# Splitting float64 dense weights and scaling softmax rows in a fused attention and two-layer MoE kernel: which engine does three of its steps

## The chip, the cores and the metric

One core of one Trainium2 chip runs the whole program. The metric is the device time of one execution in microseconds; below it the profile's own span is named where it is used. The engines have short names in the profile: PE (matmul), DVE (VectorE), ACT (ScalarE), POOL (GpSimd), SP (which issues most of the DMAs).

## The reference

```python
# attention: q, k, v are (4, 8, 576, 64); causal window of 128, ALiBi-like bias
scores = scale * q @ k.T; scores = where(mask, scores + bias, -1e9)
attn = exp(scores - max); attn = attn / (attn.sum(-1) + 1e-9)
x = (attn @ v)                      # as (2304, 512)
# dense layer: w_in (512, 2048) and w_out (2048, 512) are float64
h = x @ w_in; g = h * sigmoid(1.702 * h); x = g @ w_out
# sparse layer: 8 experts, one per token by argmax(x @ w_gate), skipped where x @ w_skip <= 0
y = gate * (relu(x @ w1[e]) @ w2[e]); out = x + y on the tokens that are not skipped
```

## The kernel before

The 2304 tokens are 18 tiles of 128 rows; two tiles make a chunk of 256 columns for the dense layer. The dense layer's hidden width is 16 slices f of 128, and each slice of weights is held as a high and a low part in the matmul's fp32 format, so that a product is three matmul passes (high x high, high x low, low x high).

**Weights of the dense layer.** They arrive as float64, read as pairs of 32-bit words. `issue` loads slice f of w_in and w_out into one of four staging tiles `stg` (SP's queue), and `tick` turns a staged slice into a pair of tiles h (high) and l (low). There are 21 such units: slices 0 to 10 whole (128 partitions x 1024) and slices 11 to 15 in two halves (128 x 512). In `tick` the steps are, in this order: ACT takes the absolute value of the high words into a scratch tile (L508); the low words are scaled by 2 to the power -29 (L510 on POOL for the slices of the tuple `LOP`, five of them, L513 on ACT for the others); DVE clamps (L514), shifts and masks (L516), combines the sign bit (L518) and adds the low words as integers (L520); ACT copies the float32 value, rounded, to h (L522); POOL subtracts h from the value and writes l (L523). At its end `tick` issues up to two more loads. All 21 units are done in the first part of the run, during the first tiles' attention and the first two chunks' dense layer.

**Attention.** `job_s` makes the scores of four heads of a tile: matmuls, masking on DVE (L318), a running minimum with the bias (L340, DVE), four exponentials with their sums (L345, ACT), the sum plus 1e-9 and its reciprocal (L347, L348, DVE) and the scaling of the four blocks by it. For tiles 0 to 3 (`full(t)`) the scaling is four instructions of 128 x 128 on POOL (L351), 32 in all; for the others it is one broadcast multiply on POOL (L354). `job_pt` transposes the scaled rows on PE (L364), copies them on ACT (L289 or L371) and cuts the two triangles on POOL (L376, L380). `job_pv` multiplies by v and writes the dense layer's input xT (ACT L411, DVE L412).

**Dense layer.** `mm1` multiplies xT by w_in (L610), applies the activation (ACT L615, DVE L616, ACT L618, DVE L619); `mm2` multiplies by w_out (L685). `main` runs them over pairs of slices and calls jobs of the next tiles in between, from the list `fill`.

**What sets the order.** The source gives an order by calls (the lists `BO`, `mix` and `fill`); a scheduler that simulates the engines with estimated durations then fixes the order in each engine's queue and puts the semaphores in. Each engine runs its queue in order. The chunks 0 and 1 run half of their slices early (`HJ`), and the rest when the later slices are ready; chunks 2 to 8 and the sparse layer come after that, with all dense weights in place.

Of the kernel before, what the change touches and what calls it, by code (L numbers as in the profile page):

```python
# [11 lines left out]
F32 = mybir.dt.float32  # L12
# [3 lines left out]
U32 = mybir.dt.uint32  # L16
I64 = mybir.dt.int64
I8 = mybir.dt.int8
AF = mybir.ActivationFunctionType
ALU = mybir.AluOpType  # L20
# [9 lines left out]
def kernel(  # L30
# [13 lines left out]
    nc = tc.nc  # L44
# [15 lines left out]
    scale = 1.0 / float(D) ** 0.5  # L60
# [105 lines left out]
    def kind_of(t):  # L166
        g = t * P
        if g % S == 0:
            return "first"
        if g // S != (g + P - 1) // S:  # L170
            return "split"
        if (g - P) // S != g // S:
            return "after"
        return "plain"
# [45 lines left out]
    def full(t):  # L220
        return t < NB
# [71 lines left out]
    def job_s(t, g):  # L293
        c = 1 if full(t) else t % 2
        kind = kind_of(t)
        if boot[0] and g == 0:
            ps = [ps_y.tile([P, 2, 2, P], F32, tag=f"y{r}", name="sps") for r in range(2)]
        else:
            ps = [ps_s.tile([P, 2, 2, P], F32, tag=f"s{r}", name="sps") for r in range(2)]
        for j in range(2):  # L300
            p = 2 * g + j
            w = slice(c, c + 1) if t == 0 else slice(0, 2)
            if full(t):
                for r in range(2):
                    nc.tensor.matmul(ps[r][:, j, w], qf[0][half[r], t, p, :],
                                     kf[0][half[r], p, max(t - 1, 0):t + 1],
                                     start=True, stop=True)
                continue
            for r in range(2):
                nc.tensor.matmul(ps[r][:, j, w], qT[t][:, r, p, :], kT[:, r, p, w],  # L310
                                 start=True, stop=False)
            for r in range(2):
                nc.tensor.matmul(ps[r][:, j, w], qlo[:, r, p, :], kT[:, r, p, w],  # L313
                                 start=False, stop=True)

        def put(p0, p1, n, data):
            for r in range(2):
                nc.vector.copy_predicated(  # L318
                    out=ps[r][p0:p1, :, c, 0:n],
                    mask=mlo[p0:p1, 0:n].unsqueeze(1).to_broadcast([p1 - p0, 2, n]),  # L320
                    data=ps[r][p0:p1, :, 1 - c, 0:n] if data is None
                    else data[p0:p1].unsqueeze(1).to_broadcast([p1 - p0, 2, n]))

        h2 = P // 2
        if kind == "first":
            put(0, P, P, big)
        elif kind == "split":
            put(0, h2, P, None)
            put(h2, P, P, big)
            for r in range(2):  # L330
                nc.vector.memset(ps[r][h2:P, :, c, 0:h2], BIG)
        else:
            put(0, P, P, None)
            if kind == "after":
                put(0, P, h2, big)
        x = ap2.tile([P, 4, P], F32, tag="e", name="e")
        mn = rp.tile([P, 4], F32, tag="mn", name="mn", bufs=2)
        sm = rp.tile([P, 4], F32, tag="sm", name="sm", bufs=2)
        for hh in range(4):
            nc.vector.tensor_tensor_reduce(out=x[:, hh, :], in0=ps[hh % 2][:, hh // 2, c, :],  # L340
                                           in1=alibi[:, 2 * g + hh // 2, :],
                                           scale=odd if hh % 2 else 1.0, scalar=3.0e38,
                                           op0=ALU.add, op1=ALU.min, accum_out=mn[:, hh:hh + 1])
        for hh in range(4):
            nc.scalar.activation(out=x[:, hh, :], in_=x[:, hh, :], func=AF.Exp, scale=-1.0,  # L345
                                 bias=mn[:, hh:hh + 1], accum_out=sm[:, hh:hh + 1])
        nc.vector.tensor_scalar_add(sm, sm, 1e-9)  # L347
        nc.vector.reciprocal(out=sm, in_=sm)  # L348
        if full(t):
            for hh in range(4):  # L350
                nc.gpsimd.tensor_scalar(out=x[:, hh, :], in0=x[:, hh, :], scalar1=sm[:, hh:hh + 1],  # L351
                                        scalar2=1.0, op0=ALU.mult, op1=ALU.mult)
        else:
            nc.gpsimd.tensor_tensor(out=x, in0=x, in1=sm.unsqueeze(2).to_broadcast([P, 4, P]),  # L354
                                    op=ALU.mult)
        eT[t, g] = x
# [58 lines left out]
    def boot_jobs(t):  # L415
        jobs = {
            "s0": lambda: job_s(t, 0),
            "s1": lambda: job_s(t, 1),
            "v": lambda: job_v(t),
            "q": lambda: t + 1 < NB and job_q(t + 1),  # L420
            "k": lambda: t + 1 < NB and job_k(t + 1),
            "p0": lambda: job_pt(t, 0),
            "p1": lambda: job_pt(t, 1),
            "o0": lambda: job_pv(t, 0),
            "o1": lambda: job_pv(t, 1),
        }
        return [jobs[z] for z in BO]
# [18 lines left out]
    NSTG = 4  # L446
    BST = (4, 7, 8)
    BO = ('s0', 's1', 'v', 'q', 'k', 'p0', 'p1', 'o0', 'o1')
    LOP = (2, 3, 4, 6, 8)
    stg = []  # L450
    stgof = []
    units = []
# [14 lines left out]
    def issue():  # L467
        i = issued[0]
        if i >= len(units) or units[i][0] >= ahead() or units[i][0] >= len(stgof):
            return  # L470
        issued[0] += 1
        f, sl = units[i]
        st = stgof[f][:, sl]
        if not wide:
            st = st.rearrange("p s d t -> p s (d t)").bitcast(F32)[:, :, 0:DM]
        staged[i] = st
        for j, s in enumerate(range(sl.start, sl.stop)):
            if s == 0:
                pat = "(k p) f t -> p k (f t)" if wide else "(k p) f -> p k f"
                dst = "p (k f) t -> p k (f t)" if wide else "p (k f) -> p k f"  # L480
                nc.sync.dma_start(
                    out=st[:, j].rearrange(dst, k=KD),
                    in_=w_in[:, f * P:(f + 1) * P].rearrange(pat, p=P))
            else:
                nc.sync.dma_start(out=st[:, j], in_=w_out[f * P:(f + 1) * P, :])

    def tick():
        i = ticked[0]
        if i >= len(units):
            return  # L490
        ticked[0] += 1
        f, sl = units[i]
        if (-1, f) not in wt:
            wt[-1, f] = wp.tile([P, 2, 2, DM], F32R, tag="w", name="w")
        h = wt[-1, f][:, 0, sl, :]
        l = wt[-1, f][:, 1, sl, :]
        x = staged.pop(i)
        if wide:
            lo, hi = x[:, :, :, 0], x[:, :, :, 1]
            if f < NFULL:  # L500
                if scr[0] is None:
                    scr[0] = wp.tile([P, 2, 2, DM], F32, tag="w", name="scr")
                c = scr[0][:, scr[1] % 2]
                scr[1] += 1
            else:
                c = yp.tile([P, 1, DM], F32, tag="b", name="wc")
            ci = c.bitcast(I32)
            nc.scalar.activation(out=c, in_=hi.bitcast(F32), func=AF.Abs)  # L508
            if f in LOP:
                nc.gpsimd.tensor_scalar(out=lo, in0=lo.bitcast(U32), scalar1=2.0 ** -29, scalar2=1.0,  # L510
                                        op0=ALU.mult, op1=ALU.mult)
            else:
                nc.scalar.activation(out=lo, in_=lo.bitcast(U32), func=AF.Copy, scale=2.0 ** -29)  # L513
            nc.vector.tensor_scalar(out=c, in0=c, scalar1=HI_MAX, scalar2=HI_MIN, op0=ALU.min,  # L514
                                    op1=ALU.max)
            nc.vector.tensor_scalar(out=ci, in0=ci, scalar1=3, scalar2=0x3FFFFFF8,  # L516
                                    op0=ALU.logical_shift_left, op1=ALU.bitwise_and)
            nc.vector.scalar_tensor_tensor(out=ci, in0=hi, scalar=-0x40000000, in1=ci,  # L518
                                           op0=ALU.bitwise_and, op1=ALU.bitwise_or)
            nc.vector.tensor_tensor(out=hi, in0=ci, in1=lo, op=ALU.add)  # L520
            x = hi.bitcast(F32)
        nc.scalar.activation(out=h, in_=x, func=AF.Copy)  # L522
        nc.gpsimd.tensor_tensor(out=l, in0=x, in1=h.bitcast(F32), op=ALU.subtract)  # L523
        for _ in range(2):
            issue()

# [825 lines left out]
```

## Time and profile before

| what | value |
|---|---|
| three runs | 809.61 us median, 808.86 to 810.9 |
| profiled execution | 808.83 us, of which the profile's span is 807.1 us |
| mean granted PE clock | 0.959 |
| busy: PE, PE weight loads | 739.3 us (92%), 656.5 us (81%) |
| busy: DVE, ACT, POOL | 520.9 us (65%), 381.7 us (47%), 382.4 us (47%) |

Busy time is the time in which an instruction of the engine is under way, waiting for a port included; it doesn't count the time before an instruction's semaphores are set. Line numbers (L523) are those of the kernel before. In a row of a stretch the busy times stand in the order PE, PE weight loads, DVE, ACT, POOL (or only the engine of the line asked for), each with its number of instructions, and behind them the granted PE clock as a share of full speed, the DMA share and GB/s. In a row of a group of instructions the name left of the arrow is what is written, the names right of it what is read.

### The profile page before, as it was taken

What the parts mean: (1) busy time and instruction counts of PE and PEld (TensorE: products, weight loads), DVE (VectorE), ACT (ScalarE), POOL (GpSimd) and SP (SyncE); (2) the same over time, 40 slices, a digit from 0 to 9 for tenths busy, and PEclk for the clock granted to TensorE, in tenths of its full rate; (3) what the DMA queues carried; (4) which work ended last, traced back from release to release, by engine and by line L of the source; (5) the groups of instructions that cost most, each with busy time, mean ns of one, the idle gap of its engine ahead of it and who ended that gap; (6) DMA issues with size and microseconds to landing.
All of it is one profiled execution on the core that took longest, in us unless ns stands there. A gap on an engine that the chain in (4) does not pass through costs nothing.

```text
span 807.1 us, 14142 instructions
## 1 busy us (share of the span) xinstructions
PE 739.3 (92%) x5087; PEld 656.5 (81%) x5087; DVE 520.9 (65%) x1195; ACT 381.7 (47%) x828; POOL 382.4 (47%) x386
## 2 busy tenths in 40 slices
PE   5658679899999999999999999999998996999994
PEld 4437469699989989999999999989987775998883
DVE  5999999954646557557557656556377537656541
ACT  4567565543444535544535544544354334545420
POOL 3699943532434326126226226227046147679540
PEclk9686889999999999999999999999999997999997
DMA  9933373111211211211211211200454177688600
GB/s 247 257 105 105 104 196 119 27 66 48 85 28 27 79 28 37 69 27 39 68 27 32 74 28 39 68 14 2 172 195 130 53 225 279 227 265 281 197 14 22
DMA packets 106151, 82.80 MB, mean 103 GB/s; under 512 B 63098, under 2 KB 83706, under 8 KB 106080
## 3 DMA queue, kind: packets, MB, share of 16 engines
q1 hardware_dynamic: 102224, 76.05, 31.6%
q0 software_dynamic: 2656, 5.67, 2.1%
q8 instruction: 41, 0.67, 0.3%
q10 hardware_dynamic: 1200, 0.17, 0.2%
q14 instruction: 30, 0.25, 0.1%
HBM read 68.98 MB, written 14.06 MB: 103 GB/s over the span
## 4 chain that ended last, share of the span: by engine, by line
PE 65%; DVE 8%; POOL 8%; issue 8%; DMA 6%; SPq 4%; ACT 1%; POOLq 0%; DVEq 0%; ACTq 0%
PE hps L610 25%; PE y L685 23%; PE ops L406 5%; POOL e L351 2%; DMA st<-in_moe_w_dram 2%; POOL w L538 2%; SPq L192 2%; PE sps L310 2%; PE hps L640 2%; PE sps L313 2%; PE pps L364 1%; PE y L670 1%; POOL w L523 1%; PE ltps L743 1%; DMA stg<-in_moe_w_in_dram 1%
## 5 line engine op out<-in xcount | busy, mean ns | idle before, releaser
L685 PE MATMUL y<-w,g 128*128 128x512 f32 x1008 | 262.1, 399 | 1.8 <-ACT g L618 1.4
L610 PE MATMUL hps<-xT,w 128*128 128x256 f32 x1728 | 240.6, 289 | 11.1 <-ACT xT L411 4.4
L610 PEld LDWEIGHTS hps<-xT,w 128*128 128x128 f32 x1728 | 225.0, 194 | 18.2 <-ACT xT L411 4.8
L685 PEld LDWEIGHTS y<-w,g 128*128 128x128 f32 x1008 | 180.7, 190 | 34.9 <-ACT g L618 1.6
L538 DVE TENSOR_TENSOR w<-st,w 128x1024 fp32r<-128x1024 f32 x38 | 66.5, 1772 | 34.5 <-ACT w L534 31.8
L616 DVE SCALAR_TENSOR_TENSOR th<-th,hps 128x512 f32<-128x512 f32 x72 | 49.3, 684 | 53.0 <-ACT th L615 52.5
L345 ACT ACTIVATE e<-e,mn 128x128 f32<-128x128 f32 x144 | 56.4, 393 | 51.1 <-DVE mn L340 50.9
L376 POOL TENSOR_SCALAR_AFFINE_SELECT pT<-pT 128x512 fp32r<-128x512 f32 (+1 forms) x64 | 46.3, 723 | 71.9 <-ACT pT L371 71.2
L615 ACT ACTIVATE th<-hps 128x512 f32<-128x512 f32 x72 | 43.0, 597 | 68.6 <-PE hps L610 55.1
L619 DVE TENSOR_TENSOR g<-th,g 128x512 fp32r<-128x512 f32 x72 | 58.5, 812 | 25.8 <-ACT g L618 24.7
L534 ACT ACTIVATE w<-st 128x1024 fp32r<-128x1024 f32 x51 | 53.2, 1057 | 35.5 <-PE y L685 12.8
L538 POOL TENSOR_TENSOR w<-st,w 128x1024 fp32r<-128x1024 f32 x26 | 67.5, 2608 | 4.3 <-ACT w L534 2.9
L618 ACT ACTIVATE g<-th 128x512 fp32r<-128x512 f32 x72 | 45.4, 631 | 40.8 <-DVE th L616 40.5
L354 POOL TENSOR_TENSOR e<-e,sm 128x512 f32<-128x512 f32 x28 | 29.2, 1044 | 70.5 <-DVE sm L348 33.7
L523 POOL TENSOR_TENSOR w<-stg,w 128x1024 fp32r<-128x1024 f32 (+1 forms) x19 | 39.9, 2102 | 19.7 <-ACT w L522 19.7
L99 POOL TENSOR_SCALAR qT<-qT 64x512 fp32r<-64x512 f32 x28 | 18.6, 663 | 62.6 <-ACT qT L240 62.0
L380 POOL TENSOR_SCALAR_AFFINE_SELECT pT<-pT 128x512 fp32r<-128x512 f32 (+1 forms) x58 | 43.7, 754 | 9.2 <-DVE pT L372 6.2
L412 DVE TENSOR_TENSOR xT<-ops,xT 64x256 fp32r<-64x256 f32 x72 | 29.7, 414 | 25.8 <-ACT xT L411 25.2
L670 PE MATMUL y<-w,g 128*128 128x512 f32 x168 | 43.9, 410 | 0.4 <-DVE o L1179 0.4
L411 ACT ACTIVATE xT<-ops 64x256 fp32r<-64x256 f32 x72 | 27.0, 375 | 34.3 <-DVE xT L412 15.9
L640 PE MATMUL hps<-w,gx 128*128 128x512 f32 x168 | 42.8, 399 | 0.2 <-ACT gx L1171 0.2
L406 PE MATMUL ops<-pT,vS 128*64 128x128 f32 x648 | 42.4, 222 | 0.0
(192 smaller groups left out, 1206.8 us busy)
## 6 DMA issues: line engine op xcount, KB each, us to landing
st<-in_moe_w_dram SPq DMA_DIRECT2D x40, 512.0 KB, 4.7
st<-in_moe_w_dram SPq DMA_DIRECT2D x48, 256.0 KB, 4.5
stg<-in_moe_w_in_dram SPq DMA_DIRECT2D x15, 512.0 KB, 4.9
stg<-in_moe_w_out_dram SPq DMA_DIRECT2D x15, 512.0 KB, 4.9
out_dram<-ys SPq DMA_DIRECT2D x18, 256.0 KB, 3.1
y_dram<-ys SPq DMA_DIRECT2D x18, 256.0 KB, 3.3
q<-in_q_dram SPq DMA_DIRECT2D x12, 256.0 KB, 2.8
k<-in_k_dram SPq DMA_DIRECT2D x12, 256.0 KB, 3.1
```

The source lines that it names most:

```text
L345: nc.scalar.activation(out=x[:, hh, :], in_=x[:, hh, :], func=AF.Exp, scale=-1.0, bias=mn[:, hh:hh + 1], accum_out=sm[:, hh:hh + 1])
L376: nc.gpsimd.affine_select(out=y[:, 0, a], in_=f32(y[:, lo, a]), pattern=[[0, 4], [1, P]], compare_op=ALU.is_ge, fill=0.0, base=0, channel_ ...
L406: nc.tensor.matmul(ps[0:64, hh % 2, hh // 2, :], vS[tt][:, a, h, :], y[:, sel, b, hh, :], start=(i == 0), stop=(i == n - 1))
L523: nc.gpsimd.tensor_tensor(out=l, in0=x, in1=h.bitcast(F32), op=ALU.subtract)
L534: nc.scalar.activation(out=h, in_=st, func=AF.Copy)
L538: eng.tensor_tensor(out=l, in0=st, in1=h.bitcast(F32), op=ALU.subtract)
L610: nc.tensor.matmul(ps[:, fi], w[:, a, 0, kk * P:(kk + 1) * P], x[:, b, kk, :], start=(i == 0), stop=(i == 3 * KD - 1))
L616: nc.vector.scalar_tensor_tensor(out=th, in0=th, scalar=1.0, in1=ps, op0=ALU.add, op1=ALU.mult)
L619: nc.vector.tensor_tensor(out=g[:, 1], in0=th, in1=g[:, 0].bitcast(F32), op=ALU.subtract)
L640: last = nc.tensor.matmul(ps, x[:, b, kk, i * P:(i + 1) * P], wa[p[0], fh, a][:, kk, :], start=(n == 0), stop=(n == 3 * KD - 1))
L670: nc.tensor.matmul(yps[p][i], g[:, a, f, :], w[:, b, f % 2, :], start=(fh == 0 and f == 0 and n == 0), stop=(fh == NH - 1 and f == 3 and n ...
L685: nc.tensor.matmul(yps[key][i], g[:, a, fi, i * P:(i + 1) * P], w[:, b, 1, :], start=(j == js[0] and fi == 0 and n == 0), stop=(j == js[-1 ...
```

## The change

Three edits. The subtraction that makes the low part l in `tick` goes from POOL to DVE (21 instructions). The scaling of the low words is on ACT for all slices (five of the wide units were on POOL). The scaling of the softmax rows of tiles 0 to 3 goes from POOL to ACT (32 instructions).

```diff
         if full(t):
             for hh in range(4):
-                nc.gpsimd.tensor_scalar(out=x[:, hh, :], in0=x[:, hh, :], scalar1=sm[:, hh:hh + 1],
-                                        scalar2=1.0, op0=ALU.mult, op1=ALU.mult)
+                nc.scalar.activation(out=x[:, hh, :], in_=x[:, hh, :], func=AF.Copy,
+                                     scale=sm[:, hh:hh + 1])
...
-    LOP = (2, 3, 4, 6, 8)
...
-            if f in LOP:
-                nc.gpsimd.tensor_scalar(out=lo, in0=lo.bitcast(U32), scalar1=2.0 ** -29, scalar2=1.0,
-                                        op0=ALU.mult, op1=ALU.mult)
-            else:
-                nc.scalar.activation(out=lo, in_=lo.bitcast(U32), func=AF.Copy, scale=2.0 ** -29)
+            nc.scalar.activation(out=lo, in_=lo.bitcast(U32), func=AF.Copy, scale=2.0 ** -29)
...
         nc.scalar.activation(out=h, in_=x, func=AF.Copy)
-        nc.gpsimd.tensor_tensor(out=l, in0=x, in1=h.bitcast(F32), op=ALU.subtract)
+        nc.vector.tensor_tensor(out=l, in0=x, in1=h.bitcast(F32), op=ALU.subtract)
```

## Rows read from the trace of the kernel before

**Rows 1.** Stretches: from:to, length, busy us by engine, granted clock, DMA share, GB/s

```profile
0.00:38.00 38.00, 21.03 (x93) 15.80 (x94) 28.66 (x70) 18.78 (x47) 18.48 (x39) 0.86 1.09 267
...
38.00:91.00 53.00, 35.43 (x174) 27.56 (x173) 50.78 (x94) 34.85 (x72) 51.47 (x43) 0.73 0.29 100
...
91.00:163.00 72.00, 60.59 (x374) 53.07 (x373) 68.38 (x119) 43.64 (x89) 37.76 (x29) 0.95 0.39 112
...
200.00:807.00 607.00, 585.20 (x4169) 526.04 (x4168) 354.03 (x872) 270.27 (x588) 263.61 (x262) 0.98 0.31 94
...
38.00:163.00 125.00, 96.03 (x547) 80.63 (x546) 119.16 (x212) 78.49 (x160) 89.23 (x71) 0.85 0.34 107
```

**Rows 2.** Chain of waits, in order of time: start, length, what

```profile
61.00 3.00 POOL w L523
...
119.75 1.40 DVE wc L518
```

**Rows 3.** Stretch 38:163, DVE alone; lines L518, L520, L514, L516, L619, L347 in order

```profile
38.00:163.00 125.00, 28.11 (x18) 0.85 0.34 107
...
38.00:163.00 125.00, 19.72 (x19) 0.85 0.34 107
...
38.00:163.00 125.00, 16.03 (x18) 0.85 0.34 107
...
38.00:163.00 125.00, 14.14 (x18) 0.85 0.34 107
...
38.00:163.00 125.00, 8.07 (x9) 0.85 0.34 107
...
38.00:163.00 125.00, 4.54 (x7) 0.85 0.34 107
```

**Rows 4.** The same for POOL's lines L523, L351, L510 in order

```profile
38.00:163.00 125.00, 37.26 (x19) 0.85 0.34 107
...
38.00:163.00 125.00, 21.20 (x24) 0.85 0.34 107
...
38.00:163.00 125.00, 7.17 (x4) 0.85 0.34 107
```

**Rows 5.** Single instructions of DVE and POOL in order of time: start, length

```profile
38.01 0.15 DVE L347 TENSOR_SCALAR sm<-sm 128x4 f32<-128x4 f32 x1
...
52.04 2.40 POOL L523 TENSOR_TENSOR w<-stg,w 128x1024 fp32r<-128x1024 f32 x1
...
52.76 2.77 DVE L518 SCALAR_TENSOR_TENSOR scr<-stg,scr 128x1024 int32<-128x1024 int32 x1
...
56.96 1.21 DVE L520 CUSTOM_DVE_ANT_0 stg<-stg,scr 128x2048 uint16<-128x2048 uint16 x1
...
58.25 0.68 DVE L516 TENSOR_SCALAR scr<-scr 128x1024 int32<-128x1024 int32 x1
...
59.60 1.18 DVE L518 SCALAR_TENSOR_TENSOR scr<-stg,scr 128x1024 int32<-128x1024 int32 x1
...
125.69 0.41 DVE L514 TENSOR_SCALAR wc<-wc 128x512 f32<-128x512 f32 x1
...
129.41 0.67 DVE L518 SCALAR_TENSOR_TENSOR wc<-stg,wc 128x512 int32<-128x512 int32 x1
...
162.11 1.32 POOL L523 TENSOR_TENSOR w<-stgx,w 128x512 fp32r<-128x512 f32 x1 [2.95 <-ACT w L522]
```

**Rows 6.** Groups by line: ACT in 38:91 (two), DVE in 91:163 (one)

```profile
L345 ACT ACTIVATE e<-e,mn 128x128 f32<-128x128 f32 x16 | 6.2, 393 | 0.7 <-DVE mn L340 0.7
...
L513 ACT ACTIVATE stg<-stg 128x1024 int32<-128x1024 uint32 x4 | 4.6, 1151 | 0.0
...
L619 DVE TENSOR_TENSOR g<-th,g 128x512 fp32r<-128x512 f32 x8 | 7.3, 912 | 1.6 <-ACT g L618 1.6
```

**Rows 7.** Waits of 0:163: who for whom, us in all, times, longest

```profile
POOL w L523 <- ACT w L522: 24.9, 9, 5.3
...
ACT w L522 <- DVE stg L520: 20.9, 12, 3.9
```

## The prediction

> **What bounds the kernel now.** The first view is the table of stretches [rows 1]. From 200 us to the end PE is busy 585.20 of 607.00 us, so there PE sets the pace. Before that it does not: in 38 to 163 us PE has 96.03 us of work in 125.00. In 38 to 91 us DVE (50.78 of 53.00) and POOL (51.47) are both full; in 91 to 163 us DVE alone is (68.38 of 72.00). ACT has room in both. The second view, the chain of waits, says the same in order of time [rows 2]: around 60 us the chain runs along POOL (3.00 us of it one subtraction at L523), around 120 us along DVE (1.40 us of one L518). Every edited instruction lies in these first 163 us: 21 subtractions at L523, 32 scalings at L351 and 5 at L510, of which 19, 24 and 4 fall in 38 to 163 us [rows 4]. What this stretch gets shorter or longer should pass on whole to the end, since PE has no gap behind it to absorb a shift.
>
> The third view, single instructions in order of time, shows that DVE's 119.16 busy us [rows 1] are not 119 us of work [rows 5]. The bit operation at L518 on 128x1024 takes 1.18 us at 59.60, and 2.77 us at 52.76, where POOL's subtraction began at 52.04 and held until 54.44: 1.68 us of waiting for POOL, then about 1.1 of work. A L347 on four numbers per partition takes 0.15 us when nothing is in its way, and 4.54 us for seven of them [rows 3], or 0.65 each. So a POOL instruction that touches SBUF charges DVE's SBUF instructions for the rest of its hold.
>
> **The change, part by part,** for 38 to 163 us.
>
> DVE's waiting for POOL. Undisturbed durations [rows 5]: L518 1.18 wide and 0.67 on 128x512, L520 1.21 (narrow as L518), L516 0.68, L514 0.41 narrow (the two alike), L347 0.15, L619 as a narrow L518. Of the L518, L520, L514 and L516 in the stretch 8 are wide and 10 narrow (one more L520 only ends in it). Busy less undisturbed [rows 3]: L518 28.11 - (8 x 1.18 + 10 x 0.67 = 16.1) = 12.0; L520 19.72 - (9.7 + 6.7) = 3.3; L514 16.03 - (5.4 + 4.1) = 6.5; L516 14.14 - 9.5 = 4.6; L619 8.07 - 9 x 0.67 = 2.0; L347 4.54 - 1.1 = 3.4. Together 31.8 us.
>
> How much of it goes. POOL loses 37.26 (L523) + 21.20 (L351) + 7.17 (L510) = 65.63 of its 89.23 busy us [rows 1, 4]; 26% stay, the triangle selections and the few copies. If the waiting falls with POOL's busy time 8.3 us of it stay, and if L523's long holds made it all, none. I take the middle, 4.2, because the long stalls that I can see begin inside an L523; both ends go into the range. Term: -27.6.
>
> The subtractions on DVE. Two SBUF inputs, fp32, like L518 and L520: 9 wide x 1.21 + 10 narrow x 0.67 [rows 5] = +17.6.
>
> New waits on DVE. The subtraction needs ACT's copy (L522) just before it. POOL waited for that copy 24.9 us in 9 waits [rows 7], but POOL had little else to do late in the stretch. The nearest case on DVE is L619 behind ACT's L618: 1.6 us before 8 of them in 91 to 163 us [rows 6], 0.20 each; 19 x 0.20 = +3.8. Lower end 0 (other DVE work is in front), upper end 7.6 (twice that, since L522 copies twice as many elements as L618 where the slice is wide). Queued behind a waiting subtraction are the clamps and bit operations of the next weight slice, and the softmax minima, for which ACT and PE wait.
>
> ACT's new work: 24 scalings of 128x128, at L345's 0.39 at most, and 4 low-word scalings at L513's 1.15 [rows 6]: 9.4 + 4.6 = 14.0 us, all of it in 38 to 91 us, where ACT goes from 34.85 to 48.9 of 53.00 [rows 1]. I cost it at 0, covered by ACT's 18 idle us; if that cover is gone it is the second rival. PE's transposes of the scaled rows (L364) come no later for it, and PE is not what ends this stretch: 0 gain too.
>
> Queues. The edits move no DMA between queues. SP's loads of the next weight slices wait until the staging tile has been read by the subtraction; POOL reached it late (it was full), DVE should reach it sooner. Taken as 0. In 0 to 38 us the DMA share is 1.09 [rows 1], so loads lead there: two subtractions cost DVE 2.4 and spare it at most two holds of 2.40 [rows 5], so the ends are +2.4 and -2.4, taken as 0.
>
> The order in each queue is planned ahead from estimated durations, so it may differ in places; in 200 to 807 us no edited instruction runs, hence 0 there.
>
> Sum: -27.6 + 17.6 + 3.8 = -6.2 us (DVE's 119.16 becomes about 109, plus its waits). The profiled execution took 808.83 us (span 807.10), 0.78 under the median 809.61 of the three runs. 808.83 - 6.2 = 802.6.
>
> On such an exchange the Trainium skill speaks against the change: Perfetto Trace Analysis, section Optimizing Scalar/DVE Operations, says that GpSimd and VectorE share an SBUF read port, so moving operations between the two might not help. Rows 5 agree that they block each other; whether the exchange is even is the first rival. By the rule taken strictly, nothing is won and the time stays near 808.8.
>
> **The rivals.**
>
> First, an even exchange: DVE takes on what it stops waiting for. The whole 8.3 us of waiting stays and the new waits come to 7 (between 3.8 and 7.6): -31.8 + 8.3 + 17.6 + 7 = +1.1, so 809.9, no change. For it: the selections that stay on POOL read SBUF too, and now find more two-input work on DVE. Against: on the narrow tile L518's own time is half that of POOL's subtraction, so the pair holds shorter. Chance 0.16.
>
> Second, slower: ACT becomes the bound in 38 to 91 us. Each scaling waits in ACT's queue for DVE's reciprocal, and behind it stand the copies (L522) and absolute values (L508) that feed DVE. ACT would have 48.9 us of work in a stretch of 53.00, so it decides from 4.1 us of idle time on; now it is idle 18.15. If 14 of these remain the stretch takes 62.9, +9.9; the later stretch still gains what I ascribe to it, about half of 6.2, or -3.1. Together +6.8: 815.6; the point of no change lies near 7 us of remaining idle time. For it: ACT now waits 20.9 us at L522 for DVE's L520 [rows 7]. Against: that wait is longest where DVE is stalled by POOL. Chance 0.18.
>
> Third, more gained: all of the waiting goes and the new waits hide. -31.8 + 17.6 = -14.2: 794.6. Chance 0.10.
>
> **How the numbers follow.** The forecast has 0.56: 802.6, its own range 798.4 (4.2 us more, the other end of the waiting) to 806.4, where it is 0.3% (2.4 us) under the profiled time; less than that a measurement of this kernel can't tell from no change. Faster by over 0.3% is the forecast and the third rival: 0.66. Same is the first rival, 0.16; slower is the second, 0.18. The range must reach to the even exchange and partly into each outer case: 795 to 813.
>
> **What would show it.** In the changed profile, over 38 to 163 us or what becomes of it: POOL's busy time down by about 66; L518 wide near 1.2 mean and L347 near 0.15 to 0.3; a DVE subtraction of 1.2 wide and 0.67 narrow; DVE busy near 109; the last subtraction starting near 157 instead of 162.11 [rows 5]; PE's full stretch beginning that much earlier and then unchanged to the end. ACT's idle time in the first half of it tells the second rival: waits of ACT's scaling for L348 of 1 us or more, eight times, with DVE idle behind them. The prediction is wrong if L518 stays long with POOL idle, for then the waiting was never POOL's; if the subtraction itself takes near 1.8 wide; or if the stretch shrinks and PE gives the time back later.

## The result, and the profile after

The changed kernel took 799.88 us in the median of four runs (795.02 to 800.86) against 809.24 us (808.62 to 810.9) for the kernel before, run beside it: a ratio of 0.9874, 95% interval 0.984 to 0.9907. That is 9.4 us, between 7.5 and 12.9 by the interval. The forecast was 6.2 us and the range 795 to 813. The profiled execution took 799.3 us with a span of 797.2.

From here on lines after L449 have moved: up to L509 by one, from L514 on by five. What were L508, L514, L516, L518, L520, L522 and L523 are L507, L509, L511, L513, L515, L517 and L518 in the changed kernel.

First the stretches, in the columns of [rows 1]. For the kernel before, up to the end of its last subtraction (162.11 + 1.32 = 163.43 us, [rows 5]) and from there to the store of the second chunk's result (210.18 us):

```profile
0.00:163.43 163.43, 117.49 (x640) 96.78 (x641) 147.90 (x283) 97.70 (x209) 108.13 (x110) 0.85 0.52 145
...
163.43:210.18 46.75, 46.75 (x356) 42.66 (x356) 27.87 (x80) 18.57 (x46) 14.33 (x19) 1.00 0.17 52
```

For the changed kernel, the first two of the old stretches and a part of the second (40 to 80 us), then up to the end of its last subtraction (156.57 us) and to the same store (201.13 us):

```profile
0.00:38.00 38.00, 21.57 (x104) 16.34 (x104) 28.57 (x80) 25.93 (x63) 8.22 (x28) 0.80 1.09 267
...
38.00:91.00 53.00, 37.79 (x203) 30.54 (x204) 52.34 (x102) 47.51 (x102) 13.26 (x12) 0.76 0.36 122
...
40.00:80.00 40.00, 26.20 (x146) 21.50 (x146) 39.54 (x87) 39.36 (x87) 8.98 (x8) 0.76 0.46 158
...
0.00:156.57 156.57, 117.28 (x692) 98.76 (x692) 139.45 (x316) 113.18 (x253) 36.70 (x57) 0.86 0.54 150
...
156.57:201.13 44.56, 42.91 (x299) 38.72 (x300) 24.11 (x62) 17.15 (x40) 9.47 (x13) 0.96 0.19 58
```

Up to the last subtraction 6.86 us are gone: DVE's busy time fell from 147.90 to 139.45 us (8.45 less), and its idle time rose from 15.53 to 17.12 (1.59 more). From there to the second chunk's store another 2.19 us are gone, since less of PE's work was left over (356 matmuls in 46.75 busy us before, 299 in 42.91 after). POOL is nearly empty (108.13 us busy up to the last subtraction before, 36.70 after by the same view), and between 40 and 80 us ACT is nearly full, 39.36 of the 40 us, with DVE at 39.54. ACT never stood idle in front of one of its new scalings:

```profile
L351 ACT ACTIVATE e<-e,sm 128x128 f32<-128x128 f32 x32 | 10.3, 409 | 0.0
```

Then DVE's lines (columns as in [rows 6]), up to the end of the weights' preparation. Before:

```profile
L518 DVE SCALAR_TENSOR_TENSOR scr<-stg,scr 128x1024 int32<-128x1024 int32 x11 | 19.1, 1735 | 0.1
...
L514 DVE TENSOR_SCALAR scr<-scr 128x1024 f32<-128x1024 f32 x11 | 13.9, 1264 | 2.2 <-ACT scr L508 2.2
...
L518 DVE SCALAR_TENSOR_TENSOR wc<-stg,wc 128x512 int32<-128x512 int32 x8 | 10.1, 1266 | 0.1
...
L347 DVE TENSOR_SCALAR sm<-sm 128x4 f32<-128x4 f32 x11 | 6.0, 548 | 0.8 <-ACT e L345 0.8
```

After:

```profile
L513 DVE SCALAR_TENSOR_TENSOR scr<-stg,scr 128x1024 int32<-128x1024 int32 x11 | 14.2, 1287 | 0.0
...
L509 DVE TENSOR_SCALAR scr<-scr 128x1024 f32<-128x1024 f32 x11 | 7.9, 723 | 0.7 <-ACT scr L507 0.6
...
L513 DVE SCALAR_TENSOR_TENSOR wc<-stg,wc 128x512 int32<-128x512 int32 x8 | 5.5, 681 | 0.0
...
L347 DVE TENSOR_SCALAR sm<-sm 128x4 f32<-128x4 f32 x12 | 3.3, 277 | 0.9 <-ACT e L345 0.9
...
L518 DVE TENSOR_TENSOR w<-stg,w 128x1024 fp32r<-128x1024 f32 x11 | 13.6, 1233 | 1.4 <-ACT w L517 1.4
...
L518 DVE TENSOR_TENSOR w<-stg,w 128x512 fp32r<-128x512 f32 x8 | 5.5, 692 | 0.1
```

The wide L518 (now L513) fell from 1735 to 1287 ns, the wide L514 (now L509) from 1264 to 723, the narrow L518 from 1266 to 681, and L347 on its four numbers from 548 to 277. The subtraction takes 1233 wide and 692 narrow on DVE, and it waits 1.5 us in all for ACT's copy.

Last, where the gain is made. The store of a chunk's result (SP's queue, start and length; each of the nine chunks has two, and the later one is shown), for the second chunk and the eighth. Before:

```profile
210.18 0.45 SPq L709 DMA_DIRECT2D out_dram<-ys  x1
```

```profile
578.74 0.47 SPq L709 DMA_DIRECT2D out_dram<-ys  x1
```

After:

```profile
201.13 0.45 SPq L704 DMA_DIRECT2D out_dram<-ys  x1
```

```profile
570.30 0.69 SPq L704 DMA_DIRECT2D out_dram<-ys  x1
```

The lead is 9.05 us at the second chunk and 8.44 at the eighth: what was gained by 210 us was kept through six chunks in which PE sets the pace. In the profiled executions what follows the eighth store, the ninth chunk and the sparse layer, gives 1.5 us more (span less the eighth store: 228.4 before, 226.9 after). No edited instruction runs there, and the four runs of the changed kernel alone are 5.8 us apart. How much of a total can come from there is seen below, among the experiments.

### The profile page after: what moved, and what is told of

Its sections match the earlier page's. It is cut to its first block, busy times and chain, and to the rows that moved or that the text cites. A ratio compares the mean times of both kernels' runs of the same rounds, so it can differ in the third digit from the quotient of the medians.

```text
span 797.2 us, 14128 instructions
## 1 busy us (share of the span) xinstructions
PE 734.8 (92%) x5087; PEld 653.1 (82%) x5087; DVE 512.4 (64%) x1216; ACT 395.9 (50%) x865; POOL 308.7 (39%) x328
## 4 chain that ended last, share of the span: by engine, by line
PE 63%; DVE 11%; DMA 7%; issue 7%; ACT 5%; POOL 3%; SPq 2%; POOLq 0%; ACTq 0%; DVEq 0%
PE hps L605 23%; PE y L680 23%; PE ops L406 5%; DMA stg<-in_moe_w_out_dram 2%; DMA st<-in_moe_w_dram 2%; DVE w L533 2%; PE hps L635 2%; PE sps L310 1%; PE pps L364 1%; PE sps L313 1%; POOL w L533 1%; PE ops L401 1%; DMA y_dram<-ys 1%; PE ltps L738 1%; ACT stg L508 1%
## 5 line engine op out<-in xcount | busy, mean ns | idle before, releaser
L533 DVE TENSOR_TENSOR w<-st,w 128x1024 fp32r<-128x1024 f32 x38 | 69.9, 1859 | 32.2 <-ACT w L529 29.6
L533 POOL TENSOR_TENSOR w<-st,w 128x1024 fp32r<-128x1024 f32 x26 | 69.2, 2673 | 5.3 <-ACT w L529 3.9
L99 POOL TENSOR_SCALAR qT<-qT 64x512 fp32r<-64x512 f32 x28 | 18.6, 665 | 84.1 <-ACT qT L240 65.8
L406 PEld LDWEIGHTS ops<-pT,vS 128*64 128x64 f32 x648 | 42.0, 135 | 0.8
```

What stands on the lines that cost most here:

```text
L406: nc.tensor.matmul(ps[0:64, hh % 2, hh // 2, :], vS[tt][:, a, h, :], y[:, sel, b, hh, :], start=(i == 0), stop=(i == n - 1))
L533: eng.tensor_tensor(out=l, in0=st, in1=h.bitcast(F32), op=ALU.subtract)
```

## The experiments

Call the edits A (subtraction to DVE), B (all low words to ACT) and C (softmax rows of tiles 0 to 3 to ACT). The change is A, B and C. Each run was timed beside the kernel before, whose median was 808.5 to 809.2 us. "The theory" is that of the prediction: a POOL instruction holds DVE's instructions up until it ends (a hold), so DVE waited. Each edit lets the scheduler plan the queues anew, so a variant differs from its neighbour in more than the edit.

**A alone.** LOP and the scaling at L351 as in the kernel before:

```diff
-        nc.gpsimd.tensor_tensor(out=l, in0=x, in1=h.bitcast(F32), op=ALU.subtract)
+        nc.vector.tensor_tensor(out=l, in0=x, in1=h.bitcast(F32), op=ALU.subtract)
```

> Only the subtraction goes to DVE; the low words of five slices and the softmax rows stay on POOL. Theory (DVE waited for POOL's long subtractions; giving them up is worth more than the 17.6 us of new DVE work): most of the change's 9.4 us comes with this edit alone, 801 to 804 us, and ACT is not full anywhere. First rival (POOL's queue in 38 to 91 us was the bound, and any 30 us off POOL would do): about as much as with the other two edits alone. Second rival (ACT's new work costs something): this kernel is faster than the full change, 797 or less.

Measured: 797.22 us, ratio 0.9868 (0.9848 to 0.9889). The whole of the change's gain, and more than the theory's 801 to 804; the time lies at the edge of the second rival's 797 or less. The stretch from 40 to 80 us of it, and that up to its last subtraction (columns as in [rows 1]):

```profile
40.00:80.00 40.00, 29.31 (x151) 22.52 (x149) 39.69 (x84) 29.21 (x63) 34.61 (x28) 0.76 0.40 133
...
0.00:156.61 156.61, 118.24 (x692) 98.54 (x692) 142.87 (x316) 99.50 (x216) 77.09 (x94) 0.87 0.53 150
```

POOL is still 87% busy there (34.61 of 40 us), so the gain does not hang on POOL having time to spare.

**B and C without A.**

```diff
-    LOP = (2, 3, 4, 6, 8)
+    LOP = ()
...
-                nc.gpsimd.tensor_scalar(out=x[:, hh, :], in0=x[:, hh, :], scalar1=sm[:, hh:hh + 1],
-                                        scalar2=1.0, op0=ALU.mult, op1=ALU.mult)
+                nc.scalar.activation(out=x[:, hh, :], in_=x[:, hh, :], func=AF.Copy,
+                                     scale=sm[:, hh:hh + 1])
```

> The subtraction stays on POOL; the low words and the softmax rows go to ACT. Theory: POOL's long holds stay, so DVE's stalls stay but for the ones behind the four low-word scalings (some 4 us); 805 to 809 us. First rival (POOL's backlog): POOL loses 28 of its 51 busy us in 38 to 91 us, is no longer full, and the time comes near the full change, 799 to 803. Second rival: slower than before, 810 to 815, because ACT has 14 us more.

Measured: 805.23 us, 0.9968 (0.9949 to 0.9987). About 2.6 us by the ratio, inside the theory's range. POOL lost about as many busy us as in the run before (113.07 in the first 175 us of the kernel before, 78.12 with A alone, 81.27 here) and the time did not follow.

**A and B, the softmax rows still on POOL.** The diff of A and LOP = ().

> Subtraction on DVE and low words on ACT, softmax rows still on POOL. ACT has 9.4 us less than in the full change, where it was busy 19.84 of 20 us between 40 and 60 us. Theory: within 2 us of the full change (799.9), for what ACT gains DVE loses behind POOL's 128x128 scalings. Second rival (ACT is the bound there): 3 to 6 us faster than the full change, 794 to 797.

Measured: 793.14 us, 0.9818 (0.9794 to 0.9842); run again on another chip it gave 794.71, 0.9835 (0.9804 to 0.9865):

> The version with subtraction on DVE and low words on ACT once more, on the chip of these runs: 791 to 797, ratio to before 0.979 to 0.985.

So C, on top of A and B, costs 3 to 5 us by the ratios, 5 to 7 by the medians. Here the theory missed and the rival had the size about right. The last chunk's store says it with less spread. In the two profiled executions of A and B (spans 785.3 and 791.9) it stands at

```profile
611.92 0.34 SPq L709 DMA_DIRECT2D out_dram<-ys  x1
```

```profile
611.57 0.34 SPq L709 DMA_DIRECT2D out_dram<-ys  x1
```

and in those of the full change, here and in the second run below, at 619.93 and 618.35: 6 to 8 us later. The two executions of one program are 0.35 us apart there and 6.6 in the whole span, so the sparse layer alone can take 7 us more or less without any edit. Two totals that differ by a few us should be compared at this store too.

**A and C, low words of five slices on POOL.** The diff of A and of the scaling at L351.

> Subtraction on DVE and softmax rows on ACT, low words of five slices still on POOL. Theory: the low-word scalings hold POOL 1.1 to 2 us each and stall DVE's clamps and shifts, four times in the stretch: 0 to 4 us slower than the full change, 800 to 804. Second rival: ACT has 4.6 us less to do, so 2 to 4 us faster, 796 to 798.

Measured: 799.75 us, 0.9886 (0.9868 to 0.9904), the same as the full change and just under the theory's 800 to 804; the rival's 796 to 798 missed. With C in place B is worth nothing that can be measured. Without C it is worth some 4 us: A alone has 0.9848 to 0.9889, A with B 0.9794 to 0.9842.

**C alone.**

> Only the softmax rows go to ACT; subtraction and five low words stay on POOL. Theory: POOL's long holds stay and so do DVE's stalls; between before and the run with low words and softmax rows on ACT (0.9968): ratio 0.993 to 1.003. Rival (POOL's backlog ahead of PE's transposes was worth something by itself): 0.990 or less.

Measured: 806.38 us, 0.997 (0.9949 to 0.9991): no more than with B, as the theory had it. So C by itself gains a little, and costs only where A and B are in place.

**The full change again,** in the run of the next two:

> The full change once more (built from the kernel before with the same three edits), on the chip of these runs, so that they have it beside them: 798 to 802, ratio to before 0.984 to 0.991.

Measured: 799.84 us, 0.9885 (0.9862 to 0.9907).

**POOL's holds put back, with nobody waiting for them.** In the changed kernel, `dmp` being a new scratch tile:

```diff
         nc.vector.tensor_tensor(out=l, in0=x, in1=h.bitcast(F32), op=ALU.subtract)
+        w_ = sl.stop - sl.start
+        nc.gpsimd.tensor_tensor(out=dmp[:, 0:w_], in0=h.bitcast(F32), in1=h.bitcast(F32), op=ALU.subtract)
```

> The changed kernel, and behind each of DVE's 21 subtractions POOL does a subtraction of the same size (h minus h into a scratch tile that nobody reads, so nobody waits for it). Theory (a POOL instruction that reads SBUF holds DVE's SBUF instructions up for the rest of its hold): in the first 158 us L513, L509, L511, L515 and L347 of the changed kernel go back from 71.7 us towards the 100.4 us that they took before, up by 20 to 28, and the time rises by 10 us or more, to 810 or above, since DVE is full and now does the subtractions too. Rival (POOL's lateness, not its holds, was what cost time): DVE's lines stay near 72 us and the time stays at 798 to 802.

Measured: 815.32 us, 1.0064 (1.0047 to 1.008), 15.5 us over the full change of the same chip (the profiled execution, 821.23 us, was the longest of seven). DVE's lines of this kernel (L514, L510, L348 and L519 are the changed kernel's L513, L509, L347 and L518), up to 175 us:

```profile
L514 DVE SCALAR_TENSOR_TENSOR scr<-stg,scr 128x1024 int32<-128x1024 int32 x11 | 18.0, 1639 | 0.0
...
L510 DVE TENSOR_SCALAR scr<-scr 128x1024 f32<-128x1024 f32 x11 | 9.4, 859 | 0.9 <-ACT scr L508 0.9
...
L348 DVE TENSOR_SCALAR sm<-sm 128x4 f32<-128x4 f32 x11 | 5.4, 488 | 0.5 <-ACT e L346 0.5
...
L519 DVE TENSOR_TENSOR w<-stg,w 128x1024 fp32r<-128x1024 f32 x11 | 18.5, 1686 | 1.2 <-ACT w L518 1.2
```

The first goes back from 1287 to 1639 ns, the softmax sum (L348) from 277 to 488, and the subtraction itself from 1233 to 1686. Over all shapes, the five lines that I named take 83.7 us (71.7 in the changed kernel), and the subtraction 28.66 (20.91): +19.7 us together. I had expected 20 to 28 from the five lines alone, and they gave 12.0; the expected time, 810 or above, came. The last subtraction ends at 175.16 us, 18.6 later than in the changed kernel. One such collision, in order of time:

```profile
66.96 1.90 POOL L521 TENSOR_TENSOR dmp<-w 128x1024 f32<-128x1024 f32 x1 [6.66 <-ACT w L518]
...
67.06 2.87 DVE L514 SCALAR_TENSOR_TENSOR scr<-stg,scr 128x1024 int32<-128x1024 int32 x1
```

POOL's subtraction starts at 66.96, and L514, which takes 1.2 undisturbed, starts 0.1 us later and takes 2.87: 1.80 until POOL is done, then 1.07 of work. POOL was not late with anything that PE needs: PE's weight loads waited 3.2 us for the triangle selections in all, 6.8 in the changed kernel. This shows the mechanism for the subtractions: their holds alone cost the time, whoever needs the result.

**Does C cost because ACT is full?** In the version with A and B, 32 copies into a new scratch tile `dmp` that nobody waits for:

```diff
         if full(t):
+            for hh in range(4):
+                nc.scalar.activation(out=dmp[:, hh, 0:P], in_=x[:, hh, :], func=AF.Copy)
             for hh in range(4):
                 nc.gpsimd.tensor_scalar(out=x[:, hh, :], in0=x[:, hh, :], scalar1=sm[:, hh:hh + 1],
```

> The version with subtraction on DVE and low words on ACT (793.1) and, behind each group of four exponentials of tiles 0 to 3, four copies of 128x128 on ACT into a scratch tile that nobody waits for, 32 in all, 10 us of ACT time. Theory (ACT has no room between 38 and 80 us, so any 10 us there costs what the softmax scaling cost): 797 to 801, near the full change. Rival (the scaling costs because it waits in ACT's queue for DVE's reciprocal): it stays at 791 to 795.

Measured: 801.19 us, 0.9896 (0.9863 to 0.993), 0.2 us above the range of the first of the two. But half of C costs the same:

```diff
             for hh in range(4):
-                nc.gpsimd.tensor_scalar(out=x[:, hh, :], in0=x[:, hh, :], scalar1=sm[:, hh:hh + 1],
-                                        scalar2=1.0, op0=ALU.mult, op1=ALU.mult)
+                if hh < 2:
+                    nc.gpsimd.tensor_scalar(out=x[:, hh, :], in0=x[:, hh, :],
+                                            scalar1=sm[:, hh:hh + 1], scalar2=1.0,
+                                            op0=ALU.mult, op1=ALU.mult)
+                else:
+                    nc.scalar.activation(out=x[:, hh, :], in_=x[:, hh, :], func=AF.Copy,
+                                         scale=sm[:, hh:hh + 1])
```

> Subtraction on DVE, low words on ACT, of each four softmax blocks two scaled on POOL and two on ACT. If ACT's room in 38 to 80 us is what the full change lacks, half of the scalings on ACT cost about half of the 6.7 us between the full change and the version without them: 795 to 798. Rival (ACT has enough room for half of them and POOL's queue gets shorter): 789 to 793.

Measured: 801.25 us, 0.9896 (0.9863 to 0.9928). Both sides of this expectation fell. The stretches of this kernel:

```profile
40.00:80.00 40.00, 27.43 (x144) 22.51 (x144) 39.84 (x86) 36.19 (x77) 17.94 (x16) 0.71 0.45 156
...
90.00:100.00 10.00, 8.53 (x56) 7.05 (x55) 3.95 (x8) 6.60 (x14) 0.88 (x2) 1.00 0.59 184
```

ACT has 3.8 us to spare between 40 and 80 us, DVE is as full as ever, and yet the time is that of the full change. Where it goes is in the second row: between 90 and 100 us DVE works 3.95 of 10 us. The full change has the same hole (first row; the second is used below), and the version with A and B has not:

```profile
90.00:100.00 10.00, 9.34 (x66) 8.49 (x66) 5.18 (x10) 6.41 (x12) 0.81 (x1) 1.00 0.95 288
...
160.00:170.00 10.00, 10.00 (x59) 9.12 (x59) 4.57 (x8) 2.63 (x6) 0.00 (x0) 0.87 0.27 105
```

```profile
40.00:80.00 40.00, 28.44 (x161) 23.79 (x162) 39.75 (x86) 32.75 (x67) 30.32 (x29) 0.77 0.39 132
...
90.00:100.00 10.00, 7.78 (x51) 7.39 (x51) 9.81 (x17) 6.97 (x12) 0.93 (x1) 0.83 0.72 218
...
160.00:170.00 10.00, 10.00 (x68) 8.83 (x67) 4.02 (x8) 3.29 (x7) 0.00 (x0) 1.00 0.27 105
```

In the full change DVE stands idle there while ACT, which prepares its input, waits for the next slices to land (2.92 us of it at one stretch). SP's queue, the wait of its weight loads for the subtraction that frees a staging tile (us in all, times, longest), and the two loads around the longest:

```profile
SPq L480 <- DVE w L518: 43.8, 6, 12.7
```

```profile
75.39 0.37 SPq L480 DMA_DIRECT2D stg<-in_moe_w_in_dram  x1
...
89.10 0.37 SPq L480 DMA_DIRECT2D stg<-in_moe_w_in_dram  x1
```

For 13.7 us no weights are asked for. In the version with A and B the same gap between loads is 12.4 us (78.22 to 90.58), but DVE has other work then, and works 9.81 of 10 us. Up to the last subtraction DVE is idle 17.12 us in the full change and 10.8 with A and B (141.65 busy of 152.45), against 2.2 us less of busy time: that is 4.1 us of the 6.3 that lie between the two second-chunk stores (201.13 and 194.82). The rest is behind the last subtraction. In the full change PE has a gap at its first matmuls after the last subtraction, and its mean granted clock from 160 to 170 us is 0.87, which lies between its two levels, 1.2 and 2.4 GHz; with A and B it is 1.00 [see the two last rows above]. The gap (time, length, and in brackets the idle time before):

```profile
158.22 4.04 PE L605 MATMUL hps<-xT,w 128*128 128x256 f32 x21 [2.91 <-DVE th L611]
```

What makes the order of the work leave DVE that hole is not settled. The scheduler plans each kernel's queues anew, and C, half of C and the idle copies all gave an order with DVE short of work near 95 us (5.18, 3.95 and 7.10 of 10 us). I have no run that holds the order and adds ACT's work alone.

Nor do the hole, the gap and the clock explain C's cost. A alone, where ACT has none of the new work, has no hole, and has the same gap and clock:

```profile
90.00:100.00 10.00, 8.86 (x62) 8.04 (x61) 9.15 (x15) 7.32 (x12) 0.76 (x1) 1.00 0.58 180
...
160.00:170.00 10.00, 10.00 (x60) 9.23 (x60) 4.42 (x8) 2.46 (x5) 0.00 (x0) 0.88 0.28 105
```

```profile
158.25 4.63 PE L610 MATMUL hps<-xT,w 128*128 128x256 f32 x24 [3.69 <-DVE th L616]
```

Yet its second chunk's store, at 201.29 us, is as late as that of the full change (201.13). A with C works 9.27 of those 10 us on DVE and stores at 199.52, half of C stores at 199.75, the idle copies at 201.35. Of these versions only A with B (194.82, and 194.58 the second time) is clearly earlier. Whether that is ACT's room or a lucky order stays open.

**Two more places for the softmax scaling,** both with A and B: one broadcast multiply on POOL, as the later tiles have it, and DVE.

```diff
-            for hh in range(4):
-                nc.gpsimd.tensor_scalar(out=x[:, hh, :], in0=x[:, hh, :], scalar1=sm[:, hh:hh + 1],
-                                        scalar2=1.0, op0=ALU.mult, op1=ALU.mult)
+            nc.gpsimd.tensor_tensor(out=x, in0=x, in1=sm.unsqueeze(2).to_broadcast([P, 4, P]),
+                                    op=ALU.mult)
```

> The version with subtraction on DVE and low words on ACT, with the softmax rows of tiles 0 to 3 scaled on POOL by one broadcast multiply of 128x512 (1.04 us elsewhere in the kernel) in place of four of 128x128 (four times 0.37 when undisturbed, 0.98 each in that version). Theory: fewer holds, each longer: within 2 us of 793.1. A rival would be 3 us or more gained, for POOL's 8 x 0.5 us come ahead of PE's transposes.

Measured: 795.39 us, 0.9824 (0.9791 to 0.9857), level with A and B; the second chunk's store lies at 197.53 us, later than theirs.

```diff
-                nc.gpsimd.tensor_scalar(out=x[:, hh, :], in0=x[:, hh, :], scalar1=sm[:, hh:hh + 1],
-                                        scalar2=1.0, op0=ALU.mult, op1=ALU.mult)
+                nc.vector.tensor_scalar(out=x[:, hh, :], in0=x[:, hh, :], scalar1=sm[:, hh:hh + 1],
+                                        scalar2=None, op0=ALU.mult)
```

> Subtraction on DVE, low words on ACT, and the softmax rows of tiles 0 to 3 scaled on DVE (32 instructions of 128x128) in place of POOL. DVE is full between 38 and 80 us, so what it is given there costs its own time less the stalls that POOL's scalings made: 32 x 0.15 to 0.25 = 5 to 8 us added, 2 to 6 us of stalls gone. Theory: 792 to 798. Rival (POOL's scalings still stall DVE by much): 788 to 791.

Measured: 798.87 us, 0.9875 (0.9841 to 0.9908), just beyond the slow end of what I had expected. The 32 instructions take 7.30 us on DVE, and up to the last subtraction DVE is 3.5 us busier than with A and B (145.13 against 141.65): on the full engine they cost more than the stalls that they save.

The best version here is A with B, the change without its third edit; by total time the single multiply can't be told from it.

## Why the prediction was right, point by point

*What bounds the kernel.* Right. The stretch after 200 us kept its length within 0.6 us between the second and the eighth store (368.56 before, 369.17 after), so what was gained ahead of it was kept.

*DVE's waiting for POOL, -27.6.* Right in mechanism, a little too large. Over the whole preparation L518, L514, L516, L520 and L347 took 100.4 us before and take 71.7 after; with the prediction's undisturbed durations they would take 64.6, so 35.8 us of waiting fell to 7.1. In the stretch and the six lines for which the term was worked out (L619 with them, from 38 us to the last subtraction) 90.6 us fell to 66.8: -23.9 for the forecast -27.6. About 8 us stay there, near the upper end (26%) and not the middle I took (an eighth). The run with POOL's subtractions put back shows that they cause the waiting. The runs with A alone and with B and C alone share it out: the five lines take 75.0 us with A alone and 89.9 with B and C, so A alone does nine tenths of it.

*The subtractions on DVE, +17.6.* Right: 1233 ns wide and 692 narrow, 20.91 us for all 21, where the prediction's 1.21 and 0.67 give 20.0.

*New waits on DVE, +3.8.* Too much. The wait for ACT's copy is 1.5 us, and all of DVE's idle time up to the last subtraction grew by 1.6.

*ACT's 14.0 us at no cost.* ACT's busy time up to the last subtraction rose by 15.5 us (97.70 to 113.18), and between 38 and 91 us it was busy 47.51 of 53 us, near the 48.9 of the prediction; between 40 and 80 us it was full. But the term was not 0. Against A alone the two other edits took 3.4 us off DVE's busy time (142.87 to 139.45) and put 3.4 us on its idle time (17.12 for 13.74), and the last subtraction ended at the same time (156.61 and 156.57). And without C the kernel is 3 to 7 us faster. What failed is the sentence that ACT's idle time covers the new work, or the one that a newly planned order costs nothing: the runs do not part the two.

*Queues, 0.* Right in sum, but not for the reason given, that DVE should reach the subtraction sooner than POOL. Between 36 and 130 us SP's loads waited 43.8 us for it on DVE, 12.7 at the longest. Before it was, on POOL:

```profile
SPq L481 <- POOL w L523: 46.5, 6, 11.2
```

*The sum.* The terms gave -6.2 and the last subtraction ends 6.9 us earlier. That it comes so near is in part luck: the waiting fell by 3.7 us less than forecast, which the smaller new waits (2.2) and 2.7 us less on DVE's other lines, for which there was no term, made up for. The forecast is a third under the measured 9.4 by a step that it did not have: "what this stretch gets shorter or longer should pass on whole to the end". It passed on with 2.2 us on top, because PE did more of its work inside the stretch (692 matmuls for 640) and had less left behind it. Of that lead 8.4 us were left at the eighth store and 7.8 at the ninth (627.71 and 619.93); the rest of the 9.4 lies in the sparse layer and in the spread of the runs.

*The rivals.* The even exchange, which the Trainium skill's sentence on GpSimd and VectorE (Perfetto Trace Analysis, Optimizing Scalar/DVE Operations) suggested, did not come: moving the subtraction between these two engines is the edit that pays. That POOL holds DVE up the traces do show (2.87 us for L514 beside POOL, above). The exchange is uneven because DVE was rid of 28.7 us of waiting and took on 20.9 us of work. The slower case did not come. ACT did become full, but the sign that the prediction gave for it, ACT waiting at its scalings for the reciprocal, is absent: 0.0 us before all 32.

## What to carry to other kernels

Where DVE looks full, compare the longest and the shortest instruction of one line and shape: if they differ by what is left of a POOL instruction that began earlier, DVE's busy time is partly waiting, and work taken off POOL can be put on the full engine with a gain. Test edits that come as a bundle one by one: here one of three gave the gain, and the other two together added nothing to it, though one of them alone with it did. And when queues are planned anew for each variant, a few us of difference between two variants may be the order and not the edit.

## What was not expected of the hardware

The waiting may go both ways. In the version with A and B the 32 scalings of 128x128 on POOL, 0.37 us each undisturbed and 0.80 before, take 31.92 us, or 1.00 each (stretch up to the last subtraction, columns as in [rows 4]):

```profile
0.00:152.45 152.45, 31.92 (x32) 0.90 0.55 155
```

That DVE's subtractions, which read two tiles from SBUF, now hold POOL's scalings up is the likely reading; no run tests it. One POOL instruction of four times the size, a 128x512 broadcast multiply with two inputs, costs about as much as one of these (four of them in the first 200 us before, 1042 ns):

```profile
L354 POOL TENSOR_TENSOR e<-e,sm 128x512 f32<-128x512 f32 x4 | 4.2, 1042 | 3.4 <-DVE sm L348 3.4
```

That an L347 on four numbers per partition can cost DVE 548 ns in the mean while it waits for POOL, against 0.15 us undisturbed, could be seen before the change [rows 3, 5]; that it makes up 3.4 of 31.8 us of waiting was more than I would have looked for.
